# Matmuls on zeros in several array shapes in place of half of the identity matmuls at the start

## The chip, the cores and the metric

The kernel runs on one core of one Trainium2 chip. The metric is the device time of one execution in microseconds (us). Five engines work side by side: TensorE (matmuls, PE in the profile, its weight loads PEld), VectorE (DVE), ScalarE (ACT), GpSimd (POOL), and SyncE (SP), which here issues DMAs. TensorE writes its results to PSUM, which has eight banks of 128 partitions x 512 fp32 values; the other engines read them from there.

## The reference

A layer norm, then attention (16 heads of 28, with one shared key and value head) and a two-layer MLP with relu, both on the normalised input, and their sum with the input. 2048 rows, width 448, hidden width 1792, all fp32.

```python
x = A_x                                  # (1, 2048, 448)
xn = _layernorm(x, axis=-1)
# attention
q = (xn @ wq) -> 16 heads of 28; k = xn @ wk; v = xn @ wv     # one k and v head
scores = einsum("bhqd,bkd->bhqk", q, k) * 28 ** -0.5
o = einsum("bhqk,bkd->bhqd", softmax(scores), v)
a = o.reshape(1, 2048, 448) @ wo
# MLP
b = maximum(xn @ w1, 0) @ w2
return x + a + b
```

Neither the identity matmuls at the start nor the new matmuls on zeros add anything to this result: what they write to PSUM is overwritten before it is read.

## The kernel before, in words

All in one function, `attention_plus_mlp`, with the order of the instructions of every engine written out by hand (`tc.manual_schedule()`, line 191). The work of TensorE falls into stages:

- Start (lines 199 to 230): the first rows of x are loaded in eight DMAs, GpSimd builds a 128x128 identity, and TensorE multiplies the identity by itself 24 times (`WARM`, lines 228 to 230). An fp32 matmul counts as two passes in the profile, so the profile has 48.
- Normalisation and projections (lines 465 to 520). Four blocks of 512 rows. VectorE takes the moments of a block, ScalarE, VectorE and GpSimd normalise, TensorE transposes it (`transposed`, line 372), ScalarE and VectorE take it out of PSUM as a rounded and a remainder part, and TensorE multiplies these with the projection weights (`qkv_first`, line 439, for block 0, `qkv_proj`, line 430, for the others). These matmuls use the whole array, 128 rows by 128 columns. `k_rows` (line 401) gathers the keys.
- First long stage: the MLP (`Tile`, line 712) with the row maxima of the scores (`max_mm`, line 572) and some scores. The array is split into four groups of 32 rows and 128 columns, and each group has its own matmuls, with 512 or 448 columns streamed. The order is the string `ROWS`.
- Second long stage: bursts of scores (`score_mm`, line 614, on groups of 32 rows, 28 or 30 of them used) and the product with the values (`pv`, line 832), whose four heads use all 128 rows and 32 columns each, in fp32. The order is the string `ORDER`: `V` is one call of `pv`, which is four matmuls or eight passes, `B` a burst, `O` and `f` parts of the output projection (line 872).

`bank(b)` gives PSUM bank b; 7 is called `o`. `early("m")` and `early("a")` hand out banks 3 to 6 and 0 to 2 in turn during the projections. The tile pools `hipool` and `npool` lie on the right side of SBUF; the first tile of `hipool` is filled by `load_qhi`, called after the projections of the third block (line 519).

Of the kernel before, what the change touches and what calls it, by code (L numbers as in the profile page):

```python
# [8 lines left out]
F32 = mybir.dt.float32  # L9
F32R = mybir.dt.float32r  # L10
# [6 lines left out]
NQB, NHG, HG, TPB, NKB, NPART = 4, 4, 4, 4, 16, 7  # L17
# [150 lines left out]
def attention_plus_mlp(ctx: ExitStack, tc: tile.TileContext, x, wq, wk, wv, wo, w1, w2, out):  # L168
    nc = tc.nc
    P = 128  # L170
# [4 lines left out]
    QB = 512  # L175
# [5 lines left out]
    W2C = FC * D  # L181
    SCALE = float(DH) ** -0.5
    EPS = 1e-5
    WARM = 24
    RB = 32
    KV = RB - DH
    NCH = 2 * DC + 1
# [29 lines left out]
    def bank(b):  # L217
        return psB.tile([P, QB], F32, name="o" if int(b) == 7 else f"b{b}")
# [3 lines left out]
    def early(kind):  # L222

        n = n_early[kind]
        n_early[kind] += 1
        return bank(n % 3 if kind == "a" else 3 + n % 4)

    pw = early("m")
    for _ in range(WARM):
        nc.tensor.matmul(pw[:, 0:P], ident, ident, start=True, stop=True)  # L230

    wpool = ctx.enter_context(tc.tile_pool(name="wpool", bufs=2))
    mlp = ExitStack()
# [553 lines left out]
    for c in stream:  # L787
# [3 lines left out]
        b = next(stream)  # L791
        r = (ord(c) - ord("a")) % HG
# [6 lines left out]
        elif c in "ABCD":  # L799
            r = ord(c) - ord("A")  # L800
# [134 lines left out]
    side = {"r": 0, "n": 0}  # L935
    for word in ORDER.split():
        k, a = word[0], word[1:]
        if k == "O":
            n, b = a.split(",")
# [48 lines left out]
```

## Time and profile before

| | |
|---|---|
| median of 2 runs | 995.53 us (995.23 to 995.82) |
| span of the profiled execution, which is its own time here | 996.5 us |
| TensorE busy | 989.3 us, 11684 matmul passes |
| VectorE, ScalarE, GpSimd busy | 718.0, 693.4, 249.3 us |
| identity matmuls (line 230) | 1.36 to 8.46 us, 48 passes |
| first transposes (line 372), first projections (line 439) | 9.34 us, 11.58 us |
| first call of `pv` (line 832) | 376.6 us |

In the profile, PE is TensorE, a line number such as L430 is a line of the kernel, `b` and `o` are PSUM banks. In a row of the timeline the first two numbers are start and length in us; `128*32 128x512` means that 128 rows and 32 columns of the array are used and 128x512 values are streamed. The windows give the busy time of the engines and the number of instructions that touch a window, then the clock that TensorE was granted (1.00 is full), the share of DMA and GB/s. The chain of waits is the path that set the end. The length of a single matmul in the rows holds the way through the array; what counts for the pace is the distance from start to start.

### The profile page before, as it was taken

The numbers are of one execution on the slowest core, as the hardware profiler recorded it, in microseconds if no ns is written. First come the engines' busy times: TensorE is split into PE (matmuls) and PEld (weight loads), VectorE is DVE, ScalarE is ACT, GpSimd is POOL, SyncE is SP. The second block draws the span as 40 slices with busy tenths as digits, with TensorE's granted clock in tenths as the row PEclk, the third lists the DMA queues.
The fourth block names the chain that finished last, engine by engine and source line by source line (L and its number), as shares of the span: only waits on it lengthen the run. The fifth ranks groups of instructions, "written<-read, shape, count | busy, mean of one in ns | idle before, by whom it ended". The sixth has DMA issues, their size and how long they took to land.

```text
span 996.5 us, 28729 instructions
## 1 busy us (share of the span) xinstructions
PE 989.3 (99%) x11684; PEld 631.9 (63%) x11684; DVE 718.0 (72%) x1304; ACT 693.4 (70%) x1336; POOL 249.3 (25%) x256
## 2 busy tenths in 40 slices
PE   9999999999999999999999999999999999999998
PEld 7889999999999994444444445444445433445444
DVE  7749999888798988888888876788786544743102
ACT  5633343344543457788988987889988799997994
POOL 4343465564637345010010010010110110110110
PEclk9999999999999999999999999999999999999999
DMA  7733110101010001001001002010011110000001
GB/s 234 268 138 103 44 34 22 42 14 54 6 51 3 13 3 46 22 25 46 23 25 40 28 23 70 4 46 23 24 35 33 40 34 23 14 13 28 24 13 37
DMA packets 31656, 44.04 MB, mean 44 GB/s; under 512 B 12276, under 2 KB 23220, under 8 KB 31524
## 3 DMA queue, kind: packets, MB, share of 16 engines
q1 hardware_dynamic: 24344, 32.84, 10.3%
q10 hardware_dynamic: 7180, 9.38, 3.1%
q8 instruction: 91, 1.49, 0.6%
q14 instruction: 41, 0.34, 0.1%
HBM read 29.62 MB, written 12.44 MB: 42 GB/s over the span
## 4 chain that ended last, share of the span: by engine, by line
PE 98%; DVE 1%; DMA 1%; ACT 0%; SPq 0%; issue 0%; ACTq 0%; DVEq 0%
PE o L832 25%; PE b L614 25%; PE b L712 24%; PE b L572 10%; PE b L872 4%; PE o L712 3%; PE b L430 3%; PE b L439 1%; PE b L372 1%; PE o L572 1%; DMA acc<-in_A_x 0%; PE b L401 0%; PE b L916 0%; ACT w L625 0%; PE o L430 0%; DVE nmx L576 0%
## 5 line engine op out<-in xcount | busy, mean ns | idle before, releaser
L576 DVE TENSOR_REDUCE nmx<-b 128x1 f32<-128x512 f32 x861 | 550.8, 684 | 163.3 <-PE b L572 135.0
L625 ACT ACTIVATE w<-b 128x512 f32<-128x512 f32 x1024 | 526.4, 614 | 80.1 <-PE b L614 73.1
L614 PE MATMUL b<-q,kHL 28*128 28x512 f32 (+1 forms) x3072 | 337.8, 428 | 0.4 <-ACT w L625 0.4
L572 PE MATMUL b<-kHL,qhi 28*128 28x512 f32 x911 | 324.2, 449 | 0.8 <-DVE nmx L576 0.7
L614 PEld LDWEIGHTS b<-q,kHL 28*128 28x128 f32 (+1 forms) x3072 | 194.7, 183 | 189.0 <-DVE nmx L576 104.7
L712 PE MATMUL b<-xt,w 32*128 32x512 f32 x2100 | 296.6, 392 | 0.0
L712 PE MATMUL b<-w,hH 32*128 32x448 f32 x1568 | 277.1, 368 | 0.0
L832 PE MATMUL o<-w,vtile 128*32 128x512 f32 x2048 | 269.7, 607 | 0.0
L712 PEld LDWEIGHTS b<-xt,w 32*128 32x128 f32 x2100 | 245.5, 183 | 2.2 <-issue 0.4
L712 PE MATMUL b<-w,hL 32*128 32x448 f32 x784 | 215.5, 362 | 0.0
L712 PEld LDWEIGHTS b<-w,hH 32*128 32x128 f32 x1568 | 208.0, 183 | 3.6 <-ACT y L736 0.4
L572 PEld LDWEIGHTS b<-kHL,qhi 28*128 28x128 f32 x911 | 149.0, 183 | 60.0 <-DVE nmx L576 28.5
L737 POOL TENSOR_TENSOR acc<-y,acc 128x448 f32<-128x448 f32 x112 | 127.8, 1155 | 122.1 <-ACT y L736 121.7
L856 POOL TENSOR_TENSOR on<-rb,oS 128x512 f32<-128x512 f32 x15 | 19.3, 1286 | 520.8 <-DMA rb<-rscr 278.5
L712 PEld LDWEIGHTS b<-w,hL 32*128 32x128 f32 x784 | 126.2, 183 | 0.2
L736 ACT ACTIVATE y<-b 128x448 f32<-128x448 f32 x98 | 53.0, 546 | 93.7 <-PE b L712 83.7
L832 PEld LDWEIGHTS o<-w,vtile 128*32 128x32 f32 x2048 | 42.9, 108 | 81.0 <-issue 76.6
L712 PE MATMUL o<-w,hH 32*128 32x448 f32 x224 | 65.0, 369 | 0.0
L712 PE MATMUL o<-xt,w 32*128 32x512 f32 x252 | 63.1, 392 | 0.0
L769 ACT ACTIVATE more<-b 128x512 f32<-128x512 f32 x54 | 32.2, 599 | 42.1 <-PE b L572 21.7
L712 PEld LDWEIGHTS o<-xt,w 32*128 32x128 f32 x252 | 44.5, 183 | 0.1
L727 ACT ACTIVATE hH<-b 128x512 fp32r<-128x512 f32 x50 | 29.3, 599 | 21.9 <-PE b L712 20.8
(111 smaller groups left out, 750.7 us busy)
## 6 DMA issues: line engine op xcount, KB each, us to landing
qscr<-qs SPq DMA_DIRECT2D x16, 512.0 KB
q<-qscr SPq DMA_DIRECT2D x12, 512.0 KB
rb<-rscr SPq DMA_DIRECT2D x60, 64.0 KB
out<-acc SPq DMA_DIRECT2D x16, 224.0 KB
qhi<-qscr SPq DMA_DIRECT2D x11, 256.0 KB
acc<-in_A_x SPq DMA_DIRECT2D x12, 224.0 KB
stg<-in_B_w ACTq DMA_DIRECT2D x5, 448.0 KB
q<-qscr ACTq DMA_DIRECT2D x4, 512.0 KB
```

The costliest lines, as they stand in the source:

```text
L430: nc.tensor.matmul(pq, w, xm, start=n == 0, stop=n == len(steps) - 1)
L572: nc.tensor.matmul(pm, qhi[u][rows, s * P : (s + 1) * P], k.rearrange("p k b q -> p (k b q)"), start=True, stop=True)
L576: nc.vector.tensor_reduce(dst, pm, axis=AX.X, op=ALU.max)
L614: nc.tensor.matmul(ps, keys, qst[u][rows, s, :], start=k == 0, stop=k == 2)
L625: nc.scalar.activation(p, ps, AF.Exp, scale=SCALE)
L712: mm = nc.tensor.matmul(o, w, m, start=self.left == self.n_mm - 1, stop=self.left == 0)
L727: nc.scalar.activation(hH, self.ps, AF.Relu)
L736: nc.scalar.activation(y, self.ps[:, 0:D], AF.Copy)
L737: nc.gpsimd.tensor_tensor(a, y, a, op=ALU.add)
L769: nc.scalar.activation(more, d[1], AF.Relu)
L832: nc.tensor.matmul(o_acc[u][RB * j : RB * (j + 1)], vtile[:, kb, :], ps[j], start=kb == 0, stop=kb == NKB - 1)
L872: nc.tensor.matmul(py[:, 0:D], om[:, i * P : (i + 1) * P], wm, start=n == 0, stop=n == len(steps) - 1)
```

## The change

`WARM` goes from 24 to 12. Behind the identity matmuls a 128x512 tile is taken on the right side of SBUF, cleared by VectorE, used for matmuls, and given back. `rows32` issues one matmul for each row group given: 32 rows, 128 columns, 512 streamed, in the fp32r type, each group to its own bank. `rows64` does it with a half of 64 rows. `cols32` issues four fp32 matmuls that use the rows given and 32 columns each. 60 matmuls on 32 rows, 10 on 64 rows and 36 fp32 matmuls on 32 columns (72 passes) come about in this order.

```diff
-    WARM = 24
+    WARM = 12
...
     for _ in range(WARM):
         nc.tensor.matmul(pw[:, 0:P], ident, ident, start=True, stop=True)
+    with tc.tile_pool(name="tpool", bufs=1, side="right") as tpool:
+        tw = tpool.tile([P, QB], F32R, name="tw")
+        nc.vector.memset(tw.bitcast(F32), 0.0)
+        tf = tw.bitcast(F32)
+
+        def rows32(*rs):
+            for r in rs:
+                rows = slice(RB * r, RB * (r + 1))
+                nc.tensor.matmul(bank(r), tw[rows, 0:P], tw[rows], start=True, stop=True)
+
+        def rows64(*hs):
+            for h in hs:
+                rows = slice(2 * RB * h, 2 * RB * (h + 1))
+                nc.tensor.matmul(bank(4 + h), tw[rows, 0:P], tw[rows], start=True, stop=True)
+
+        def cols32(rows, b):
+            for j in range(HG):
+                nc.tensor.matmul(bank(b)[RB * j : RB * (j + 1)], tf[rows, 0:RB], tf[rows], start=True, stop=True)
+
+        top, low, whole = slice(0, 2 * RB), slice(2 * RB, P), slice(0, P)
+        rows32(*range(HG), *range(HG))
+        rows64(0, 1, 0, 1)
+        for _ in range(3):
+            rows64(0)
+            rows32(2, 3)
+        for _ in range(3):
+            rows32(0, 1)
+            rows64(1)
+        cols32(whole, 7)
+        rows32(*range(HG), *range(HG))
+        for _ in range(2):
+            cols32(top, 6)
+            rows32(2, 3, 2, 3, 2, 3, 2, 3)
+            cols32(low, 7)
+            rows32(0, 1, 0, 1, 0, 1, 0, 1)
+        cols32(top, 6)
+        cols32(low, 7)
+        cols32(top, 6)
+        cols32(low, 7)
```

## The prediction

> **What bounds the kernel now.** I read the head of the page first, then the share of the chain by engine.
>
> ```profile
> span 996.5 us, 28729 instructions
> PE 989.3 (99%) x11684; PEld 631.9 (63%) x11684; DVE 718.0 (72%) x1304; ACT 693.4 (70%) x1336; POOL 249.3 (25%) x256
> ...
> PE 98%; DVE 1%; DMA 1%; ACT 0%; SPq 0%; issue 0%; ACTq 0%; DVEq 0%
> ```
>
> TensorE is busy for 989.3 of 996.5 us and carries 98% of the chain. Its instructions run in one written order, so work put into that order early moves everything behind it, unless TensorE was waiting at that place anyway. The change sits at the very start, so the next view is the timeline of the first microseconds and the chain there (start, length, what).
>
> ```profile
> 0.81 0.06 DVE L212 MEMSET eps_t<- 128x1 f32 x1 [0.81 <-PEq L974]
> 1.36 7.10 PE L230 MATMUL b<-ident 128*128 128x128 f32 x48 [1.36 <-POOL ident masks.py:199]
> 3.53 0.63 DVE L331 BATCH_NORM_STATS2 st<-acc 128x6 f32<-128x448 f32 x1 [2.67 <-DMA acc<-in_A_x]
> 9.34 0.75 PE L372 MATMUL b<-ident,hH 128*128 128x128 f32 x2 [0.87 <-DVE hH L358]
> 11.58 2.80 PE L439 MATMUL b<-xt,w 128*128 128x512 f32 x11
> ```
>
> ```profile
> 8.85 0.86 DVE hH L358 x2
> 9.76 2.06 PE b L372 x15
> 11.82 7.55 PE b L439 x33
> ...
> 20.73 1.75 PE b L372 x16
> ...
> 24.56 8.87 PE b L430 x39
> ```
>
> The identity matmuls (48 passes for 24 matmuls) fill 1.36 to 8.46 us. Until about 9.7 us the chain runs over the load of x and its normalisation on VectorE; from 9.76 us on it is TensorE alone. So the cover at the start is small: TensorE's transposes wait for VectorE until about 9.7 us, and from 11.58 us the projections follow without a gap. Whatever TensorE does before 9.7 us is free, and whatever goes beyond it is paid in full.
>
> **Part one, twelve identity matmuls go.** The windows over that line (second column the length, then busy time and matmuls of TensorE):
>
> ```profile
> 2.00:3.00 1.00, 1.00 (x6) 1.00 (x6) 1.00 0.88 255
> ...
> 4.00:4.50 0.50, 0.50 (x4) 0.50 (x3) 1.00 0.78 224
> 4.50:5.00 0.50, 0.50 (x7) 0.50 (x6) 1.00 0.92 246
> ...
> 6.00:7.00 1.00, 1.00 (x12) 1.00 (x11) 1.00 0.94 353
> ...
> 4.90:8.50 3.60, 3.56 (x32) 3.37 (x31) 1.00 0.92 293
> ```
>
> The pace doubles near 4.5 us (6 in one microsecond before, 12 after; a matmul that reaches over a border counts twice). The half that is left is the early one, slow part included; what goes is 24 passes at 3.56 us / 32 = 0.111 us, 2.67 us. The identity matmuls then end at 8.46 - 2.67 = 5.79 us. The faster pace is reached inside the half that stays, and the zeros follow at once, so I cost the shorter run at nothing beyond this.
>
> **Part two, the new tile and its clearing.** VectorE writes zeros to 128x512. Its nearest rows are a clearing of 128x1 in 0.06 us (above) and this one:
>
> ```profile
> L568 DVE MEMSET nmx<- 128x64 f32 x16 | 1.8, 112 | 0.0
> ```
>
> On a line through both, 512 columns take an estimated 0.49 us. It stands ahead of the first statistics, for which VectorE waits 2.67 us until 3.53 us; it is done near 1.4 us, long before TensorE wants it at 5.79 us. Without that cover it would cost its 0.49 us on the way to the normalised x. The tile's place on the right side is used again by the first preloaded queries, issued only after the third block's projections; nobody waits for it. The banks it writes are next written by TensorE itself, so no other engine gets a new wait; what is queued behind the new matmuls is all of TensorE's work.
>
> **Part three, the matmuls on zeros.** They run on the chain's engine, at 5.79 us. I count steps: a step is one matmul of 512 columns, or several on different parts of the array that start together. One alone takes 8.87 / 39 = 0.227 us (the chain's row at 24.56 us). That four on 32 rows each share such a step is shown by the long first stage:
>
> ```profile
> 110.00:360.00 250.00, 249.81 (x4370) 240.73 (x4363) 222.70 (x421) 103.45 (x188) 134.59 (x119) 1.00 0.09 26
> ```
>
> 250 / 4370 = 0.057 us each, a quarter of 0.227. For the 32-column fp32 calls and for a change of shape I take the end of the run, where both kinds stand alone:
>
> ```profile
> 978.81 0.97 PE L614 MATMUL b<-q,kHL 28*128 28x512 f32 x12
> 979.71 0.47 PE L872 MATMUL b<-woH,oH 128*128 128x448 f32 x1
> ...
> 981.73 0.97 PE L614 MATMUL b<-q,kHL 28*128 28x512 f32 x12
> 982.64 2.78 PE L832 MATMUL o<-w,vtile 128*32 128x512 f32 x24
> 985.35 0.47 PE L872 MATMUL b<-woH,oH 128*128 128x448 f32 x1
> ...
> 985.96 1.07 PE L832 MATMUL o<-w,vtile 128*32 128x512 f32 x8
> 986.95 0.47 PE L872 MATMUL b<-woH,oL 128*128 128x448 f32 x1
> ```
>
> From start to start, 8 column passes (one call) take 986.95 - 985.96 = 0.99 us and 24 take 985.35 - 982.64 = 2.71 us. So a further call costs (2.71 - 0.99) / 2 = 0.86 us, and 0.13 us is left for the change of shape. Twelve row matmuls, three steps or 0.68 us, take 0.90 and 0.91 us: 0.22 us for the change. I take the mean of both, 0.18 us; the range of a change goes from nothing (if parts that don't touch need none) to 0.22 us.
>
> No row shows a matmul on 64 rows, a column call on 64 rows, or two shapes side by side. The 64-row matmul lies between a 32-row and a 128-row one, which take the same step, so I take 0.227 us, two to a step if they are on different halves. The column call on half the rows gets 0.86 us, by the same reason. An added step cannot come out below nothing, since every pass must stream its columns.
>
> With different shapes one after the other, the steps are:
> - 8 on 32 rows: two steps, 0.45; 4 on 64 rows: two steps, 0.45
> - the two loops of 64 and 32 rows: 12 steps, of which one is shared at the seam, 11 x 0.227 = 2.50
> - one whole column call 0.86; 8 on 32 rows 0.45
> - the double loop, four times a half column call and four steps of two on 32 rows: 4 x (0.86 + 0.91) = 7.08
> - the last four half column calls, all of one shape. A call is two rounds of 0.43 us, and the order lets the second round of one run beside the first of the next: five rounds, 2.15 (four calls apart would be 3.44)
>
> That is 13.9 us. Changes of shape: one into each of the first two groups, ten in the two loops, one each into the whole call and the 32 rows after it, eight in the double loop, one into the last group and one out: 24 x 0.18 = 4.3 us. Together 18.3 us; the zeros end at 5.79 + 18.3 = 24.1 us.
>
> The Trainium skill, TensorEngine Tiling (Array Packing), section Key Properties, says that a change of tiling mode, as against a change of tile, drains the engine, and also that different tiles work in parallel. By the first the sum is the one above; by the second alone it would be that of the first rival. The 0.13 and 0.22 us agree with a drain where the shapes share the array; no run here shows it for shapes that don't.
>
> The transposes then start with all inputs there and take 1.75 us (the row at 20.73 us). Before, the projections began at 11.58 us, as if the transposes had started at 9.83 us without a wait. Delay: 24.1 - 9.83 = 14.2 us. Behind that TensorE has nothing to give back: its idle time in all is 996.5 - 989.3 = 7.2 us, of which 2.2 us lie ahead of 9.34 us, and the rest hangs on results of its own matmuls and moves along. So 996.5 + 14.2 = 1010.7 us for an execution like the profiled one, whose own time is its span; that is 1.0 us above the median of 995.53, which leaves 1009.7 us. I say 1009.5.
>
> **The rivals.**
>
> Side by side: parts of the array that don't touch work on together in different shapes. For it speaks that four row groups start together in the first stage; against it, that every change of shape in the rows above has a price. The two loops fall to 6 steps, 1.36 us; in the double loop the row matmuls start with the second column round (0.43 us) and run 0.91 us, 4 x 1.34 = 5.36 us; the rest stays (4.36 us). 11.1 us and about six changes, 1.1 us: 12.2 us, ending at 18.0 us, 8.2 us late: 1003.7 us. If matmuls could also pass each other in the double loop (4 x 0.91), 1002.
>
> Half clock, the rival on the slow side: the zeros, alone on half the array, count as too little work and the clock is halved. The trace shows such a drop in the second stage, first the windows (clock is the last column but two), then the chain there:
>
> ```profile
> 380.00:385.00 5.00, 5.00 (x34) 2.21 (x30) 4.83 (x9) 3.73 (x8) 2.07 (x2) 0.84 0.35 79
> 385.00:390.00 5.00, 4.81 (x42) 2.41 (x42) 3.82 (x10) 3.25 (x7) 1.57 (x1) 0.82 0.42 87
> 390.00:400.00 10.00, 9.82 (x101) 4.31 (x98) 9.09 (x16) 8.14 (x17) 4.14 (x2) 1.00 0.10 30
> 400.00:410.00 10.00, 9.92 (x80) 4.16 (x76) 8.02 (x14) 6.61 (x15) 0.00 (x0) 0.83 0.00 1
> ...
> 383.33 1.81 PE o L832 x8
> ...
> 388.87 1.00 PE o L832 x8
> ```
>
> A column call takes 1.81 us there against 1.00 us later. It comes where matmuls are sparse (34 in 5 us, where the first stage has 87). The two loops on half arrays have 18 matmuls in 11 x 0.227 + 10 x 0.18 = 4.3 us, as sparse in part; but TensorE streams over half of that time. If the whole of the zeros ran at half clock, 18.3 us would become 36.6 and the time 1028 us. It decides between same and slower once 5.7 us of the zeros' work run halved (1015.4 us is 2% above). The Trainium skill, TensorE: Matmul & The Clock Gate, section What's actually happening, has the gate open after a window of about 3.4 us of sustained work and close after an idle one; zeros that are issued back to back should by that count as work. The pace doubling near 4.5 us agrees; what counts as idle no run here tells finely.
>
> Nothing moves: the zeros hide. That takes an end by 9.83 us, 4.0 us of time, less than the double loop's row steps alone (16 x 0.227 = 3.6) with the whole column call. It gives 995.5 us. A little less is possible in any case: another start moves the places of the two drops of the clock, each worth about 0.8 us on a column call and as much on the rows beside it, so up to 3 us either way. For over 2% faster, 20 us, no row shows a store: TensorE's idle time after the start is 5 us.
>
> **How the numbers follow.** One after the other 0.55, side by side 0.28, half clock 0.10, hidden or nearly 0.05, a gain that I don't see 0.02. The forecast's own range goes from 24 changes at 0.1 us (1007.8) less the 3 us of the drops, to 0.22 us with four calls apart (1012): 1005 to 1012. The range for 8 in 10 takes in the side by side case and a drop of the clock for one window: 1002 to 1013. A measurement of this kernel can tell about 2% from no change. Over 2% slower is the half clock case, 0.10, and faster 0.02; the rest, 0.88, is within 2%.
>
> **What would show it.** On TensorE's timeline the identity row ends near 5.8 us and zeros run to about 24 us; the first transposes follow without a wait for VectorE, and the projections start near 26 us, 14 us later than before; from there every row of the chain stands about 14 us later with the same length. Side by side shows as row matmuls starting between two rounds of a column call, and an end near 18 us. Half clock shows as a step of 0.43 us and a column call of 1.7 us. The forecast is wrong if the shift at the first projections isn't the shift at the end, or if a stage's matmuls have another pace than before.

## The result and the profile after

The median went from 995.53 us (995.23 to 995.82) to 1074.89 us (1073.25 to 1076.54), a ratio of 1.0792 with an interval of 1.0748 to 1.0837. The forecast was 1009.5 us, within 1002 to 1013, with 0.10 for slower by over 2%. The kernel became slower by 7.9%.

The head of the page after and its chain by engine:

```profile
span 1071.4 us, 28966 instructions
PE 1062.8 (99%) x11802; PEld 645.2 (60%) x11802; DVE 717.9 (67%) x1305; ACT 693.7 (65%) x1336; POOL 249.2 (23%) x256
...
PE 98%; DVE 1%; issue 0%; DMA 0%; SPq 0%; ACT 0%; POOL 0%; POOLq 0%; DVEq 0%; ACTq 0%
```

The other engines have the busy time that they had. TensorE has 73.5 us more, for 118 passes. TensorE's timeline after shows where they are (start, length, line, array rows*columns, operands, count):

```profile
1.35 4.59 PE L230 MATMUL b<-ident 128*128 128x128 f32 x24 [1.35 <-POOL ident masks.py:199]
5.88 1.18 PE L239 MATMUL b<-tw 32*128 32x512 f32 x8
6.99 1.61 PE L244 MATMUL b<-tw 64*128 64x512 f32 x5
8.52 0.50 PE L239 MATMUL b<-tw 32*128 32x512 f32 x2
8.96 0.49 PE L244 MATMUL b<-tw 64*128 64x512 f32 x1
...
13.55 6.57 PE L248 MATMUL o<-tw 128*32 128x512 f32 x8
20.05 1.15 PE L239 MATMUL b<-tw 32*128 32x512 f32 x8
21.13 4.34 PE L248 MATMUL b<-tw 64*32 64x512 f32 x8
25.40 2.19 PE L239 MATMUL b<-tw 32*128 32x512 f32 x8
27.53 6.89 PE L248 MATMUL o<-tw 64*32 64x512 f32 x8
...
78.32 6.97 PE L248 MATMUL o<-tw 64*32 64x512 f32 x7
85.22 0.69 PE L411 MATMUL b<-ident,hH 128*128 128x128 f32 x2
...
88.55 8.53 PE L478 MATMUL b<-xt,w 128*128 128x512 f32 x33
```

The zeros start at 5.88 us, as forecast (5.79), and end at 85.22 us instead of 24.1: 79.3 us where 18.3 were expected. The first projections (line 439 before, 478 now) start at 88.55 us instead of 11.58, 77.0 us late. From there to the end the kernel is even a little shorter: 1071.4 - 88.55 = 982.9 us against 996.5 - 11.58 = 984.9. The profile before has two drops of the clock in its second long stage, to 0.82 to 0.84 between 380 and 390 us and between 400 and 410; the profile after has none behind 95 us. So all of the loss lies in the zeros and in the first transposes behind them.

A column call (line 248, eight passes) takes 4.27 us from 21.13 to 25.40 us, where the prediction had 0.86 and 0.18 for the change of shape; and the next two on 64 rows take 6.8 and 7.7 us. Two views say why. The first is that of line 248, what TensorE waited for before it (us, times):

```profile
  PE o L248: 25.6, 15
  PE b L248: 19.0, 12
  issue: 2.2, 6
```

There are 27 waits on the line's own matmuls, three in each of the nine column calls. `cols32` calls `bank(b)` for each of its four matmuls. Each call takes a new tile on the same bank, and a new tile waits until the last user of the bank is done, even if that is TensorE itself and the matmul writes other partitions. So the four matmuls of a call, which the values' product (line 832 before) sends side by side into one tile, run one behind the other. The second view is the windows over four neighbouring pieces of the double loop, two at the start and the same two later (length, then busy time and count by engine, the granted clock third from the end):

```profile
21.13:25.40 4.27, 4.10 (x11) 0.54 (x8) 0.00 (x0) 0.00 (x0) 0.00 (x0) 1.00 0.00 0
25.40:27.53 2.13, 2.02 (x10) 0.83 (x9) 0.00 (x0) 0.00 (x0) 0.00 (x0) 1.00 0.00 0
37.64:45.38 7.74, 7.57 (x10) 0.71 (x8) 0.00 (x0) 0.00 (x0) 0.00 (x0) 0.50 0.00 0
45.38:48.68 3.30, 3.19 (x10) 1.25 (x9) 0.00 (x0) 0.00 (x0) 0.00 (x0) 0.50 0.00 0
```

The same work takes 6.40 us at full clock and 11.04 at half. The clock was halved from about 12 to 18 us and again from about 29 to 90 us. The busy shares of over 90% hide both causes: a matmul's row holds its way through the array, so TensorE looks busy while one pass at a time goes through a quarter of its columns.

### The profile page after: what moved, and what is told of

The parts are those of the page before. It is cut to its first block, busy times and chain, and to the rows that moved or that the text cites. A ratio compares the mean times of both kernels' runs of the same rounds, so it can differ in the third digit from the quotient of the medians.

```text
span 1071.4 us, 28966 instructions
## 1 busy us (share of the span) xinstructions
PE 1062.8 (99%) x11802; PEld 645.2 (60%) x11802; DVE 717.9 (67%) x1305; ACT 693.7 (65%) x1336; POOL 249.2 (23%) x256
## 4 chain that ended last, share of the span: by engine, by line
PE 98%; DVE 1%; issue 0%; DMA 0%; SPq 0%; ACT 0%; POOL 0%; POOLq 0%; DVEq 0%; ACTq 0%
PE o L871 23%; PE b L751 23%; PE b L653 23%; PE b L611 9%; PE b L911 4%; PE o L248 3%; PE b L469 3%; PE o L751 3%; PE b L248 2%; PE b L239 2%; PE b L411 1%; PE b L478 1%; DVE nmx L615 1%; PE o L611 0%; PE b L230 0%; PE b L244 0%
## 5 line engine op out<-in xcount | busy, mean ns | idle before, releaser
L414 DVE TENSOR_TENSOR xt<-b,xt 128x512 fp32r<-128x512 f32 x12 | 7.7, 686 | 79.8 <-ACT xt L413 79.8
L413 ACT ACTIVATE xt<-b 128x512 fp32r<-128x512 f32 x12 | 6.5, 598 | 78.6 <-PE b L411 78.6
```

## The experiments

**e1: one tile per bank.** All zeros go to eight tiles that are taken once.

```diff
         tf = tw.bitcast(F32)
+        zb = [bank(i) for i in range(8)]
...
-                nc.tensor.matmul(bank(r), tw[rows, 0:P], tw[rows], start=True, stop=True)
+                nc.tensor.matmul(zb[r], tw[rows, 0:P], tw[rows], start=True, stop=True)
...
-                nc.tensor.matmul(bank(4 + h), tw[rows, 0:P], tw[rows], start=True, stop=True)
+                nc.tensor.matmul(zb[4 + h], tw[rows, 0:P], tw[rows], start=True, stop=True)
...
-                nc.tensor.matmul(bank(b)[RB * j : RB * (j + 1)], tf[rows, 0:RB], tf[rows], start=True, stop=True)
+                nc.tensor.matmul(zb[b][RB * j : RB * (j + 1)], tf[rows, 0:RB], tf[rows], start=True, stop=True)
```

> The changed kernel with one PSUM tile per bank for all the zeros, taken once, in place of a new tile at every matmul; the same matmuls in the same order. Theory (a new tile on a used bank makes TensorE wait for its own earlier matmul, and the waits make it sparse enough for the gate to halve the clock): the four column matmuls of a call start within 0.03 us, a call takes 0.86 us at full clock instead of 4.3, and the zeros end between 24 us (clock stays up) and 42 us (all at half clock); the time is 1008 to 1028 us, and near 1021 if the clock falls in the two sparse loops and stays down. Rival (column matmuls on this tile run one at a time by themselves): a call stays at 4.3 us or more, and the time stays above 1060 us. If shapes on different parts of the array can overlap, row matmuls start before the last round of a column call; if a change of shape empties the array, at least 0.1 us after that round's end.

Measured: 1012.28 us median of five executions (1009.97 to 1020.79), ratio 1.016 (1.0143 to 1.0178). The profiled one is the longest of them:

```profile
8.14 0.50 PE L240 MATMUL b<-tw 32*128 32x512 f32 x2
8.57 0.50 PE L245 MATMUL b<-tw 64*128 64x512 f32 x1
9.01 0.50 PE L240 MATMUL b<-tw 32*128 32x512 f32 x2
...
12.43 1.55 PE L249 MATMUL o<-tw 128*32 128x512 f32 x8
...
16.93 2.08 PE L240 MATMUL b<-tw 32*128 32x512 f32 x8
18.93 1.93 PE L249 MATMUL o<-tw 64*32 64x512 f32 x8
20.79 2.07 PE L240 MATMUL b<-tw 32*128 32x512 f32 x8
...
33.77 0.44 PE L412 MATMUL b<-ident,hH 128*128 128x128 f32 x2
```

The view of the column calls (line 249) no longer has a wait on TensorE's own matmuls, and the windows (length, busy time and count of TensorE, clock, DMA) show the clock:

```profile
  issue: 4.8, 8
```

```profile
6.00:12.00 6.00, 6.00 (x33) 1.00 0.67 175
12.00:18.00 6.00, 6.00 (x33) 0.57 0.93 280
...
24.00:30.00 6.00, 6.00 (x28) 0.50 0.00 0
30.00:42.00 12.00, 12.00 (x81) 0.86 0.00 0
```

The waits are gone and with them the long calls: 1.86 us from 18.93 to 20.79, at half clock. Column matmuls on this tile don't run one at a time by themselves; that rival is out. In this execution the clock was halved from about 13 to 33 us; two executions with a granted clock of 1.000 took 1010.19 and 1009.97 us, and those with 0.998 and 0.996 lie at 1012.28 and 1013.38. So the same kernel keeps the full clock or loses it from one execution to the next. Where it keeps it, the time is the one that the prediction gave: its sum describes this kernel, not the changed one.

The question of shapes side by side is answered too. Matmuls on rows 64 to 127 start 0.44 us behind one on rows 0 to 63, and the reverse takes 0.43 us, though TensorE waits for no other instruction between them: a step of 0.22 us and 0.2 us for the change. The weight load of the new shape, 0.18 us, starts only there too, at 8.57 us, and not ahead of it.

**e2: other data.** The tile holds rows of x.

```diff
-        nc.vector.memset(tw.bitcast(F32), 0.0)
+        nc.vector.memset(tw.bitcast(F32)[:, D:QB], 0.0)
+        nc.gpsimd.tensor_scalar(tw[:, 0:D], acc[:, 0, :], 1.0, 0.0, op0=ALU.mult, op1=ALU.add)
```

> The changed kernel, but the tile holds rows of x in 448 of its 512 columns instead of zeros (written by GpSimd), so what the matmuls compute there is other rubbish that is overwritten. Theory (the gate counts matmuls that run, whatever their data): the clock falls in the same places, the zeros' part ends near 85 us, the time is 1070 to 1078 us. Rival (matmuls on zeros hardly count as work for the gate): the clock stays at 1.00 and the time falls by some 25 us, to about 1047 us.

Measured: 1074.88 us in one execution, mean granted clock 0.967 (0.968 and 0.964 with zeros). The clock falls, comes back and falls again in the double loop, as with zeros, though the second fall comes at about 26.5 us instead of 29. The zeros' part ends 2.4 us later, at 87.60 us, and not near 85 as expected; the time is as expected. Rows of x in place of zeros don't keep the clock up here.

**e3: all rows in the column calls.**

```diff
-            cols32(top, 6)
+            cols32(whole, 6)
...
-            cols32(low, 7)
+            cols32(whole, 7)
```

(and the same in the last four calls)

> The changed kernel with all column calls on 128 rows instead of 64 (banks, number of passes and waits as before). In the changed kernel a call takes 4.27 us at full clock and 7.74 us at half, on 64 rows. If the gate counts how much of the array's rows is at work: the clock stays at 1.00 through most of the column calls, as it came back in the one call on 128 rows, and the time is 1045 to 1055 us. If it counts only whether some matmul runs: the same calls are as busy as before, the clock stays at 0.50 from about 29 to 90 us, and the time is 1070 to 1078 us.

Measured: 1046.33 us in one execution, clock 0.997. TensorE's windows of this kernel (length, busy, clock, DMA):

```profile
12.00:18.00 6.00, 5.89 (x9) 0.50 0.96 307
18.00:24.00 6.00, 5.78 (x18) 0.96 0.33 127
24.00:30.00 6.00, 5.74 (x17) 1.00 0.01 3
30.00:42.00 12.00, 11.52 (x32) 1.00 0.00 0
42.00:60.00 18.00, 17.11 (x44) 1.00 0.00 0
```

and of the changed kernel:

```profile
24.00:30.00 6.00, 5.77 (x15) 0.89 0.01 3
30.00:42.00 12.00, 11.67 (x18) 0.50 0.00 0
42.00:60.00 18.00, 17.57 (x29) 0.50 0.00 0
60.00:84.00 24.00, 23.27 (x31) 0.50 0.00 0
```

As many passes with as many waits, on 128 rows instead of 64, keep the clock at 1.00 in the double loop; a call takes 4.28 us there, as it takes 4.27 on 64 rows at full clock. A count of whether some matmul runs can't tell the two kernels apart; a count of the rows at work can. The first projections start at 62.75 us, 25.8 us earlier than in the changed kernel: about 26 us are what the second fall of the clock cost. The times differ by more, 28.6 us, but that is the median of two against one execution.

**e4: twelve identity matmuls, no zeros.**

```diff
-    WARM = 24
+    WARM = 12
```

> The kernel before with 12 identity matmuls in place of 24 and no zeros: the first part of the change alone. Prediction's step (costed at nothing): the identity matmuls end at 5.8 us, TensorE then idles 3.5 us until the transposes, time 995 to 997 us. Rival (the idle stretch closes the gate, and transposes and first projections run at half clock for one window of 3.4 us or two): 997 to 1000 us.

Measured: 999.5 us median of five (996.65 to 1000.7), ratio 1.0029 (1.0013 to 1.0045). The profiled execution's timeline and windows:

```profile
9.63 0.75 PE L372 MATMUL b<-ident,hH 128*128 128x128 f32 x2 [2.79 <-DVE hH L358]
```

```profile
6.00:9.60 3.60, 0.84 (x4) 0.55 (x3) 2.97 (x12) 1.65 (x4) 0.00 (x0) 1.00 0.75 221
9.60:11.00 1.40, 1.27 (x7) 0.87 (x8) 0.82 (x2) 0.62 (x3) 1.34 (x5) 0.89 0.30 36
11.00:14.00 3.00, 3.00 (x14) 2.81 (x14) 1.97 (x3) 2.90 (x8) 3.00 (x5) 0.50 0.76 199
```

There are 2.79 us of idle time, and then about 3.4 us at half clock over the transposes and the first projections. Two things differ from what was expected: the identity matmuls end at 6.85 us, not at 5.8, and the idle time is shorter than 3.5 us. This is one of the two shorter executions (997.42 us); its second block of transposes starts 1.9 us late (22.49 against 20.57 us). Over all executions the ratio makes it about 3 us. The first half of the change is not free by itself: the rival holds.

**e5: e1 without the two alternating loops.**

```diff
-        for _ in range(3):
-            rows64(0)
-            rows32(2, 3)
-        for _ in range(3):
-            rows32(0, 1)
-            rows64(1)
```

> The kernel of e1_one_tile without the two short loops in which matmuls on 64 and on 32 rows alternate. In e1 they take 4.3 us, and in the executions with a granted clock of 1.00 the whole took 1010 us. Theory (those loops, half of the array's rows and a gap at each change of shape, are what closes the gate; the double loop at 0.87 us a column call is dense enough to leave an open gate open): every execution has a clock of 0.998 or more and the times lie together at 1005 to 1007 us. Rival (the double loop closes the gate too): some executions have a clock of 0.99 or less and take 1010 us or more, as in e1.

Measured: 1007.74 us median of four (1005.9 to 1008.8), ratio 1.0104 (1.0087 to 1.0121). The profiled one, 1008.8 us:

```profile
7.75 1.06 PE L249 MATMUL o<-tw 128*32 128x512 f32 x8
8.74 0.74 PE L240 MATMUL b<-tw 32*128 32x512 f32 x8
9.41 1.06 PE L249 MATMUL b<-tw 64*32 64x512 f32 x8
10.40 1.19 PE L240 MATMUL b<-tw 32*128 32x512 f32 x8
11.53 1.06 PE L249 MATMUL o<-tw 64*32 64x512 f32 x8
...
19.75 0.44 PE L406 MATMUL b<-ident,hH 128*128 128x128 f32 x2
```

At full clock a column call with its change of shape takes 0.99 us and eight matmuls on two row groups 1.13 us. The double loop on half of the rows ran through at full clock in the profiled execution (1.00 in every window from 6 to 24 us), so the alternating loops are the more likely cause of the fall in e1. That isn't shown, since e1 too kept its clock in some executions; for the other executions of e5 only the mean clock is known, 0.998 and more. The profiled one has 0.996, below what was expected, and three times lie above 1007 us; its clock fell between 430 and 450 us, early in the second long stage, where the profile before has drops too. That fall is not laid to the zeros: the seven executions of the kernel before beside these runs lie between 995.1 and 998.18 us, with clocks from 1.000 to 0.996.

**e6: one tile for each column call.** The row matmuls keep a new tile each.

```diff
+            o = bank(b)
             for j in range(HG):
-                nc.tensor.matmul(bank(b)[RB * j : RB * (j + 1)], tf[rows, 0:RB], tf[rows], start=True, stop=True)
+                nc.tensor.matmul(o[RB * j : RB * (j + 1)], tf[rows, 0:RB], tf[rows], start=True, stop=True)
```

> The changed kernel with one new PSUM tile for each column call instead of one for each of its four matmuls; the matmuls on 32 and 64 rows keep their new tile each. Theory: the column calls fall from 4.27 to 0.87 us at full clock as in e1; the row matmuls keep their waits, 2.13 us for eight on two groups against about 1.0 us without, 1.1 against 0.8 for eight on four groups, some 5 us in all more than e1; and since the double loop is then two thirds sparse row matmuls on half of the rows, the gate closes in it: 1015 us if the clock stays up, 1025 to 1045 us if it falls, which I expect. Rival (the waits of the row matmuls don't matter for the gate): 1015 to 1017 us with a clock of 0.995 or more.

Measured: 1029.86 us median of four (1029.14 to 1030.0), ratio 1.033 (1.0315 to 1.0346), clock 0.983 in every execution.

```profile
17.23 1.93 PE L249 MATMUL b<-tw 64*32 64x512 f32 x8
19.09 3.36 PE L239 MATMUL b<-tw 32*128 32x512 f32 x8
22.38 1.93 PE L249 MATMUL o<-tw 64*32 64x512 f32 x8
...
41.82 0.69 PE L412 MATMUL b<-ident,hH 128*128 128x128 f32 x2
```

The row matmuls' own waits make eight of them last 3.3 us at half clock, and in the profiled execution the clock stays down from about 12.6 us until the transposes. The other three have the same mean clock and times within 0.9 us, where only one execution of five of e1 lost the clock for so long. The waits cost twice: as time, and by keeping TensorE too sparse for the full clock.

## Why the prediction was wrong

- What bounds the kernel: right. TensorE is 98% of the chain, and the loss at the first projections, 77.0 us, is the loss at the end but for 2.1 us.
- Part one: in the profile after, the identity matmuls end at 5.94 us, where they were put (5.79). There was luck in it: in the profiles of the experiments the same 24 passes end between 5.96 and 6.85 us, so the faster pace isn't always reached inside the half that stays. Costing the shorter run at nothing was right only because the zeros follow at once; alone it costs about 3 us (e4).
- Part two: here lies the step that failed. "The banks it writes are next written by TensorE itself, so no other engine gets a new wait" asked for other engines only and overlooked that a new tile makes TensorE wait for itself. Each of the helpers takes a new tile per matmul, which the diff shows. So part three put a column call at 0.86 us, taken from the values' product, where one tile serves all four matmuls; it took 4.27 us at full clock, change of shape included. With one tile per bank (e1) the median is 1012.28 us, just inside the range that was forecast.
- Part three, the counts of steps and changes: right where the waits are gone. e5's zeros take 19.75 - 6.30 = 13.45 us (its first matmul on zeros is at 6.30 us); the loops that it leaves out take 12.43 - 8.14 = 4.29 us in e1 and one step of 0.23 more. Together 18.0 us against 18.3. Term by term the misses are small: the two loops took 4.5 us for 4.3, and the last four calls 1.87 us for 2.3 with the change out, because the two halves start together. A change of shape costs 0.13 to 0.22 us.
- The terms that were missing: e3 took 61.03 - 5.89 = 55.1 us for its zeros, of which its own half clock of 6.8 us is worth about 3.4. That leaves 51.7 us at full clock, so the waits cost 51.7 - 18.0, about 34 us. From 51.7 to the 79.3 us of the changed kernel, about 28 us are the clock. The two don't simply add: without the waits, the half clock of e1's profiled execution cost only about 9 us (33.77 - 6.46 = 27.3 us of zeros). Then 1.6 us for the transposes at half clock (88.55 - 85.22 = 3.33 us where 1.75 were expected).
- Side by side: wrong as a rival. The Trainium skill, TensorEngine Tiling (Array Packing), Key Properties, says that a change of tiling mode drains the engine; e1's steps of 0.43 us on parts that don't touch agree.
- Half clock: the right mechanism at the wrong size. It was priced on 18.3 us of work, with 1028 us as its end, and given 0.10. The waits made the work 52 us long at full clock, and sparse enough for the clock to fall a second time and stay at half until 90 us. The first fall, near 12 us, needs no waits of that size: e1 has one too.
- From the profiled execution to the median: a time here is 1.8 us above its span (1073.25 against 1071.4), so the profile before belongs to an execution of about 998.3 us, not of 996.5, and the table's "its own time here" is wrong. The forecast is not hurt by it: taking off 1.0 us at the end amounts to adding the delay of 14.2 us to the median of 995.53. It does say why the medians lie 79.4 us apart and the profiled spans 74.9: the profile before is of a longer execution than its median, and the profile after of the shorter one of two.

## What to carry to other kernels

Count the waits of an engine on itself: a helper that takes a new PSUM tile for every matmul puts matmuls in a row that one tile would let run side by side, here 4.27 us instead of 0.99. Matmuls that leave rows of the array idle, or that wait on each other, also pulled the clock down here, and it stayed down until all rows were at work again; what such work costs has to be worked out at both clocks. And dummy work in front of a stage that TensorE bounds is paid in full, as soon as it lasts longer than the wait that it fills.

## What the runs showed of the hardware

What halves and restores TensorE's clock, called the gate above, goes by more than whether some matmul runs: with as many passes and waits, the double loop kept 1.00 with column calls on 128 rows (e3, one execution) and fell to 0.50 with calls on 64.

A count of the rows at work fits the loops in these profiles. These are estimates from the rows above, the share of time in which TensorE streams, times the share of rows, as means over a loop:

- e1's alternating loops, 0.22 us of every 0.43 on half of the rows: 26%, and the clock falls in the profiled execution.
- The changed kernel's double loop at full clock, (3.44 + 0.88) of 6.40 us on half of the rows: 34%, and the clock falls. The 3.44 us are the eight passes of a column call, 0.43 us each, one behind the other; the 0.88 us are four steps of row matmuls.
- e5's double loop, (0.86 + 0.88) of 2.12 us on half of the rows: 41%, and the clock stays up.
- e3's double loop, 3.44 us on all rows and 0.88 on half of about 6.40: 61%, and the clock stays up.
- e1's double loop at half clock: some 45%, and the clock doesn't come back until the two halves run together.

The changed kernel and e3, which differ in the rows of the column calls, stay apart over the sparsest 3.4 us of the double loop too, which hold all row matmuls and the start of a call: some 28% in the changed kernel and 43% in e3. A count of rows times columns doesn't fit: e3's double loop, with 32 columns in each column matmul, would be at 20% and stay up, where the alternating loops, with all columns, are at 26% and fall. The level that closes the gate seems lower than the one that opens it. Where each lies wasn't measured. The Trainium skill, TensorE: Matmul & The Clock Gate, section What's actually happening, speaks of how busy TensorE was in a window and not of rows; e3 against the changed kernel shows that rows count.

Whether the alternating loops close the gate changes from one execution to the next: e1 took 1010 us in some and 1021 us in another, with nothing changed. The alternating loops last 4.3 us, not much more than the 3.4 us for which the clock stayed halved in e4. If the gate judges stretches of that length, a whole one fits into the loops for some starts only. No run varied the start, so the cause stays open.
